# Gradient pass of a gated block: group tiles by parity, one store per weight and group, one sum over both parts of a parameter block

## The chip, the core and the metric

The kernel runs on one core of a Trainium2 chip. The metric is the time of one execution on the device in microseconds (us), taken as the median of several runs. The engines are named as in the profile: PE (TensorE, matrix multiplications; PEld is its weight load), DVE (VectorE), ACT (ScalarE), POOL (GpSimd) and SP (SyncE). POOL and SP do little arithmetic of their own here; they issue transfers (DMAs), and SP also issues transfers that transpose on the way. Each engine runs its own list of instructions in order and waits for others by semaphores. SBUF is the memory on the chip for tiles of 128 partitions, PSUM holds the results of matmuls, and tensors that are too large for them lie in DRAM.

## The reference

The kernel computes the forward pass of a block and the gradients of it with respect to 12 inputs. The input x has 2048 rows of 576 columns. The block is

```
xn = layernorm(x)
s  = conv(xn, K(A, B, C, dt)) + xn * Dskip     # state space model, as a convolution of length 2048
h  = silu(xn @ w1) * (xn @ w3)                 # 2048 x 4608
g  = silu(h @ w2)                              # 2048 x 576
out = x + s * g
```

K is a sum over 128 complex states per column, K[d, l] = Re sum_n C[d,n] exp(dt[d] A[d,n] l) dt[d] B[d,n]. The convolution is done with Fourier transforms as matrix products. Given grad_out, the outputs are out and the gradients of x, of the parameters A, B, C (real and imaginary parts), of log_dt and Dskip, and of w1, w3 and w2. With go the gradient at h @ w2, and G, U the stored xn @ w1 and xn @ w3, the part around the change is

```
gh = go @ w2.T
gu = gh * silu(G);   gg = gh * silu'(G) * U;   h = silu(G) * U
grad w2 = h.T @ go;  grad w1 = xn.T @ gg;      grad w3 = xn.T @ gu
grad xn += gg @ w1.T + gu @ w3.T
```

## The kernel before

All rows are cut into LT = 16 row tiles of 128, the 576 columns into four full chunks of 128 (nfull) and a rest of 64 (rem), and the 4608 hidden columns into NG = 18 groups of FG = 256. The program is written with tile pools: a pool gives out a fixed number of buffers (bufs) for each name, in turn, and a tile whose buffer is still in use waits for its last user. Pools lie in SBUF from the left or, with side="right", from the right, and a pool opened after another was closed may lie over the old one's place; its first writers then wait for the last readers there. The order of instructions on each engine is set by a priority: at(us) (L83) sets it for what follows, and of the instructions of each engine the smaller number goes first as far as dependences allow. So stages are interleaved by numbers given in the code, not by their place in it.

The stages, with their place in the profiled run:

- Up to about 678 us: layer norm, the convolution kernel and the forward convolution, and ffn_hidden (L725), which writes G, U and h to DRAM (G_dram, U_dram by POOL's queue, H_dram by SP's).
- 678 to 832 us: ffn_output (L800). For each row tile it loads h transposed and x_t, go_t, s_t, multiplies by w2 into two PSUM buffers po (L830), takes the sigmoid sgo on ACT (L835), and on DVE makes out, the gradient go_o and the gradient gs of s, which goes to GS_dram. PE then transposes go_o (ptr, L869), and ACT copies it to goT and goTt. Its pools o_ep and o_in lie on the left.
- 832 to about 1720 us: the groups. phase6_load (L1176) allocates and loads w2T, gg_n and h_n for a group, one group ahead, and makes silu and its derivative on ACT and two products on DVE, in quarters of a tile. phase6_group (L1201) computes ph = gh (L1220), copies it on ACT (gh, L1223), multiplies gu_n and gg_n by it on DVE (L1226), computes the gradient of w2 (phase6_grad2, matmuls L1247, copy L1251), stores gu_n and gg_n to GU_dram and GG_dram (L1232, 512 KB each, POOL's queue), and computes the gradients of w1 and w3 (phase6_grad13): for each of the two and each of the four chunks 16 matmuls into pgw (L1265), a copy to gw on ACT (L1268) and a store of 128x256 elements on POOL's queue (L1269); then a tail for the last 64 columns of both at once (L1272 to L1279).
- Beside the groups, to about 1300 us: ssm_bwd_conv (L875), the backward convolution in four quarters (conv_bwd_quarter, L916). It loads gs, multiplies it by xn for the gradient of Dskip (gsxn, L943), and makes spectra and inverse transforms (idft_tile, L596), whose first rows are halved before (L968).
- Beside the groups and the stage after them, 1300 to about 1940 us: ssm_bwd_params (L896), 36 blocks of 16 columns. param_load (L1001) brings qT, pz and the gz tiles on SP's queue two blocks ahead; param_chunk (L1013) runs small matmuls (L1023) into four PSUM tiles T of 128x512 and, for each of them and each of two parts s, one multiplication by pz into pr_q on DVE (L1030) and one sum into S_all (L1033).
- 1720 to 2065 us: phase6_inputs (L1281), the x stage. gg and gu are loaded transposed as ggc and guc, and the weights as wTB, on SP's queue, and multiplied into px (L1308). phase5_final (L1037) makes the parameter gradients from S_all beside it.

Of the kernel before, what the change touches and what calls it, by code (L numbers as in the profile page):

```python
# [11 lines left out]
ALU = mybir.AluOpType  # L12
AX = mybir.AxisListType
FP32 = mybir.dt.float32
BF16 = mybir.dt.bfloat16
I32 = mybir.dt.int32
P = 128
# [43 lines left out]
class K:  # L61
# [534 lines left out]
    def idft_tile(self, pt, V, oc, extra=()):  # L596
        nc, KT = self.nc, self.cfg.KT
        Q, Wq = V.shape[1], V.shape[4]
        sl = slice(oc * P, (oc + 1) * P)
        n = 2 * KT + len(extra)  # L600
        i = 0
        pv = pt[:, 0:Q * Wq].rearrange("p (q d) -> p q d", q=Q)
        for kt in range(KT):
            for ri, mat in enumerate((self.dC, self.dSi)):
                nc.tensor.matmul(pv, lhsT=mat[:, kt, sl], rhs=V[:, :, ri, kt, :], start=(i == 0), stop=(i == n - 1))
                i += 1
        for (lw, rh, o, w) in extra:
            nc.tensor.matmul(pt[:, o:o + w], lhsT=lw, rhs=rh, start=False, stop=(i == n - 1))
            i += 1
# [190 lines left out]
    def ffn_output(self, T0, TB):  # L800
# [11 lines left out]
        with self.tc.tile_pool(name="o_ep", bufs=2) as ep, \  # L812
                self.tc.tile_pool(name="o_in", bufs=2) as ip, \
# [61 lines left out]
    def ssm_bwd_conv(self, T0, TQ, ps):  # L875
# [3 lines left out]
        with self.tc.tile_pool(name="b_k", bufs=1, side="right") as kp, self.tc.tile_pool(name="b_z", bufs=2, side="right") as zp:  # L879
# [4 lines left out]
            nc.vector.tensor_scalar(out=self.lcol[:], in0=self.lcol[:], scalar1=1.0 / 512, scalar2=None, op0=ALU.mult)  # L884
            self.ones_col = kp.tile([P, 1], BF16, name="ones_col")
# [30 lines left out]
    def conv_bwd_quarter(self, g, kp, zp, ps, T0, TQ):  # L916
# [22 lines left out]
        for b in range(NB):  # L939
            prod = zp.tile([P, KT, W], BF16, name="gsxn")  # L940
            for tt in range(KT):
                t = b * KT + tt
                nc.vector.tensor_tensor(out=prod[:, tt, :].rearrange("p (h d) -> p h d", h=2),  # L943
                                        in0=gs[:, t, :].rearrange("p (h d) -> p h d", h=2),
                                        in1=self.nat4(self.xn_bf[:, t, :])[:, g], op=ALU.mult)
            for tt in range(KT):
                nc.tensor.matmul(gds[0:1, 0:W], lhsT=self.ones_col[:], rhs=prod[:, tt, :], start=(b == 0 and tt == 0),
                                 stop=(b == NB - 1 and tt == KT - 1))
# [7 lines left out]
        for i in range(NB - 1, -1, -1):  # L956
# [4 lines left out]
            ZZ = zp.tile([P, 1, 2, KT, W], BF16, name="ZZ")  # L961
            if nxt is not None:
                nc.vector.scalar_tensor_tensor(out=fl(ZZ), in0=fl(nxt), scalar=self.sgn[:, 0:1], in1=fl(Z), op0=ALU.mult,
                                               op1=ALU.add)
            else:
                nc.vector.tensor_copy(out=ZZ[:], in_=Z[:])
            nxt = Z
            nc.vector.tensor_scalar(out=ZZ[:, 0, :, 0, :], in0=ZZ[:, 0, :, 0, :], scalar1=self.hrow[:, 0:1], scalar2=None,  # L968
                                    op0=ALU.mult)
            for oc in range(KT):  # L970
                t = i * KT + oc
                pt = ps.tile([P, 512], FP32, name="et_ps")
                self.idft_tile(pt, ZZ, oc)
                for h in range(2):
                    pv = pt[:, h * W // 2:(h + 1) * W // 2].rearrange("p (c d) -> p c d", d=8)
                    nc.scalar.activation(out=st[:, :, 0, :, h, t], in_=pv, func=ACT.Copy, scale=1.0 / 512)
                    nc.scalar.activation(out=st[:, :, 1, :, h, t], in_=pv, func=ACT.Copy, scale=self.lcol[:, t:t + 1])
# [35 lines left out]
    def param_chunk(self, ch, tiles, S_all, qp, ps):  # L1013
# [3 lines left out]
        if True:  # L1017
            for dg in range(2):
# [7 lines left out]
                for h in range(2):  # L1026
                    d0 = h * (D // 2) + ch * 8 + dg * 4
                    for s in range(2):
                        pr = qp.tile([P, 8, 2, AV], FP32, name="pr_q")
                        nc.vector.tensor_tensor(out=pr[:], in0=T[h][:].rearrange("p r d k a -> p (r d) k a"),  # L1030
                                                in1=pz[:, dg, h, s:s + 2].rearrange("p r d a -> p (r d) a")[:, :, None, :]
                                                .to_broadcast([P, 8, 2, AV]), op=ALU.mult)
                        nc.vector.tensor_reduce(out=S_all[:, 2 * s:2 * s + 2, d0:d0 + 4].rearrange("p k d -> p d k"),  # L1033
                                                in_=pr[:].rearrange("p (r d) k a -> p d k r a", r=2), op=ALU.add,
                                                axis=AX.XY)
# [86 lines left out]
    def backward(self, T0, TG, TQ, TC, TX, gctx, mats):  # L1122
# [10 lines left out]
        with ExitStack() as out:  # L1133
            ffn = ExitStack()
            wp = ffn.enter_context(pool(name="e_w", bufs=2))
            inp = ffn.enter_context(pool(name="e_in", bufs=2))
            elp = ffn.enter_context(pool(name="e_el", bufs=3))
            gwp = ffn.enter_context(pool(name="e_gw", bufs=4))
# [37 lines left out]
    def phase6_load(self, gi, T, TG, wp, inp):  # L1176
# [7 lines left out]
        self.nat_transpose(w2T[:], self.W2_dram[gi * FG:(gi + 1) * FG, :])  # L1184
        gg = inp.tile([P, LT, FG], BF16, name="gg_n")
# [67 lines left out]
    def phase6_grad13(self, gi, gg_n, gu_n, gwp, ps_gw):  # L1253
# [7 lines left out]
        for (nat, oname) in ((gu_n, "out_11"), (gg_n, "out_10")):  # L1261
            for c in range(nfull):
# [4 lines left out]
                gw = gwp.tile([P, FG], BF16, name="gw13")  # L1267
                nc.scalar.copy(out=gw[:], in_=pw_[:, 0:FG])  # L1268
                nc.gpsimd.dma_start(out=aps[oname][c * P:(c + 1) * P, fb:fb + FG], in_=gw[:])  # L1269
# [6 lines left out]
        gw = gwp.tile([P, FG], BF16, name="gw13")  # L1276
# [192 lines left out]
```

## Time and profile before

| what | us |
|---|---|
| median of 5 runs (2087.62 to 2099.35) | 2088.8 |
| the profiled execution | 2074.07 |
| its span, first to last instruction | 2072.3 |
| PE busy | 1806.1 (87%) |
| DVE busy | 1511.9 (73%) |
| ACT busy | 965.8 (47%) |
| POOL busy | 514.3 (25%) |

The mean clock that TensorE was granted in the profiled execution is 0.956 of its full one. A row of instruction groups in the profile reads: line, engine, operation, output and inputs by their names, shapes, number of instructions | busy us in all, mean ns of one | idle us of the engine just before them, and the instruction that ended most of that idle time. In a timeline row come the start in us, the duration from the first to the last instruction of the row in us, engine, line, operation, count, and in brackets the idle time before and what released it. Among the rows that touch the change are

```profile
L1268 ACT CAST gw<-pgw 128x256 bf16<-128x256 f32 x144 | 53.3, 380 | 235.6 <-PE pgw L1265 147.3
L1269 POOL DMA_DIRECT2D out_dram<-gw x144 | 78.3, 546 | 189.3 <-ACT gw L1268 175.6
...
GU_dram<-gu_n POOLq DMA_DIRECT2D x36, 512.0 KB, 5.9
GG_dram<-gg_n POOLq DMA_DIRECT2D x36, 512.0 KB, 7.9
```

The last two are transfers: number, size of each, and the median time from issue to landing in us.

### The profile page before, as it was taken

How to read it: one execution, taken by the hardware profiler on the slowest of the kernel's cores; microseconds unless marked ns; L12 is line 12 of the kernel's file. 1: busy time of each engine (PE TensorE's matmuls, PEld its weight loads, DVE VectorE, ACT ScalarE, POOL GpSimd, SP SyncE). 2: the span in 40 equal slices, each digit the busy share in tenths (PEclk: the TensorE clock that was granted, in tenths of full speed). 3: DMA queues.
4: the chain of work that ended last, by engine and by line, in shares of the span. 5: the costliest groups of instructions: out<-in, count | busy, mean ns of one | idle time of the engine just before them, and what ended most of it. 6: DMA issues, size and time to landing. Idle time of an engine off the chain costs nothing.

```text
span 2072.3 us, 40851 instructions
## 1 busy us (share of the span) xinstructions
PE 1806.1 (87%) x16214; PEld 1253.3 (60%) x16214; DVE 1511.9 (73%) x2826; ACT 965.8 (47%) x1732; POOL 514.3 (25%) x718
## 2 busy tenths in 40 slices
PE   2889888989899999689889998889969986699997
PEld 1443333335453777577777777767747775577785
DVE  7459999997783565469595968599778874487862
ACT  1968888885455111574656657334434510000000
POOL 6015566562122211112112212323212220000000
PEclk9898999999999999799999999999989998899998
DMA  6688788877577896636372645799698779999884
GB/s 177 237 277 274 268 278 279 280 264 256 173 270 180 222 214 147 185 113 208 87 221 77 199 132 160 198 254 277 181 171 221 194 189 199 228 219 211 167 183 63
DMA packets 552113, 421.31 MB, mean 203 GB/s; under 512 B 415601, under 2 KB 482353, under 8 KB 547313
## 3 DMA queue, kind: packets, MB, share of 16 engines
q1 hardware_dynamic: 487648, 254.56, 49.3%
q0 software_dynamic: 39632, 147.49, 22.0%
q10 hardware_dynamic: 24640, 16.65, 2.9%
q8 instruction: 127, 2.08, 0.4%
q14 instruction: 66, 0.53, 0.1%
HBM read 135.96 MB, written 196.27 MB: 160 GB/s over the span
## 4 chain that ended last, share of the span: by engine, by line
PE 32%; DVE 23%; issue 16%; DMA 10%; ACT 6%; POOL 4%; SPq 2%; DVEq 0%; POOLq 0%; ACTq 0%
PE px L1308 10%; PE po L830 6%; DMA out_dram<-gw 4%; PE pgw L1265 4%; DVE pr_q L1030 4%; DVE S_all L1033 2%; DVE t_k L503 2%; SPq L1174 2%; PE pgw L1247 2%; DVE m_k L484 2%; PE ph L1220 2%; DVE q_k L490 2%; DMA gg_n<-G_dram 2%; PE et_ps L587 1%; PE pu L767 1%
## 5 line engine op out<-in xcount | busy, mean ns | idle before, releaser
L1265 PEld LDWEIGHTS <-xn_bf 128*128 128x128 bf16 x2304 | 230.0, 100 | 86.9 <-issue 53.4
L1308 PE MATMUL px<-wTB_w,guc 128*128 128x288 bf16 x1152 | 240.5, 290 | 19.2 <-DMA wTB_w<-in_B_w_dram 9.8
L1308 PE MATMUL px<-wTB_w,ggc 128*128 128x288 bf16 x1152 | 241.1, 290 | 18.2 <-DVE pr_q L1030 10.0
L1030 DVE TENSOR_TENSOR pr_q<-et_ps,pz 128x512 f32<-128x512 f32 x288 | 185.6, 682 | 93.4 <-PE et_ps L1023 88.0
L767 PEld LDWEIGHTS <-xnT 128*128 128x128 bf16 x1152 | 102.3, 99 | 173.8 <-issue 78.8
L1033 DVE TENSOR_REDUCE S_all<-pr_q 128x8 f32<-128x512 f32 x288 | 184.3, 678 | 0.2
L1220 PE MATMUL ph<-w2T,goT 128*128 128x256 bf16 x1152 | 174.9, 279 | 5.5 <-DMA w2T<-W_dram 5.5
L1265 PE MATMUL pgw<-gg_n,xn_bf 128*128 128x256 bf16 x1152 | 139.1, 283 | 40.6 <-ACT gw L1268 40.6
L1247 PE MATMUL pgw<-go_o,h_n 128*128 128x288 bf16 x1152 | 160.8, 291 | 9.6 <-DVE h_n L1198 7.5
L767 PE MATMUL pg<-wmB_w,xnT 128*128 128x512 bf16 x576 | 160.8, 388 | 2.9 <-ACT g_t L776 2.0
L1268 ACT CAST gw<-pgw 128x256 bf16<-128x256 f32 x144 | 53.3, 380 | 235.6 <-PE pgw L1265 147.3
L767 PE MATMUL pu<-wmB_w,xnT 128*128 128x512 bf16 x576 | 155.6, 387 | 2.6 <-ACT u_t L777 2.6
L499 POOL COPY pz_k<-p_k 128x256 bf16<-128x256 bf16 x144 | 135.6, 985 | 46.2 <-issue 37.1
L1265 PE MATMUL pgw<-gu_n,xn_bf 128*128 128x256 bf16 x1152 | 137.9, 277 | 8.7 <-ACT gw L1251 4.0
L830 PE MATMUL po<-w2g,hc 128*128 128x288 bf16 x1152 | 143.7, 286 | 1.3 <-ACT u_t L777 1.3
L1308 PEld LDWEIGHTS <-guc 128*128 128x128 bf16 x1152 | 113.8, 99 | 50.5 <-DMA guc<-GU_dram 10.3
L1308 PEld LDWEIGHTS <-ggc 128*128 128x128 bf16 x1152 | 113.6, 99 | 48.1 <-DMA ggc<-GG_dram 11.1
L1247 PEld LDWEIGHTS <-h_n 128*128 128x128 bf16 x1152 | 112.7, 100 | 38.4 <-DVE h_n L1198 7.7
L1220 PEld LDWEIGHTS <-goT 128*128 128x128 bf16 x1152 | 101.0, 99 | 55.0 <-issue 28.0
L830 PEld LDWEIGHTS <-hc 128*128 128x128 bf16 x1152 | 111.5, 98 | 30.3 <-issue 1.7
L1269 POOL DMA_DIRECT2D out_dram<-gw x144 | 78.3, 546 | 189.3 <-ACT gw L1268 175.6
L1354 ACT ACTIVATE t<-gx 128x576 f32<-128x576 f32 x16 | 10.9, 684 | 245.2 <-DVE gx L1318 239.4
(309 smaller groups left out, 3935.1 us busy)
## 6 DMA issues: line engine op xcount, KB each, us to landing
G_dram<-g_t POOLq DMA_DIRECT2D x72, 256.0 KB, 3.9
U_dram<-u_t POOLq DMA_DIRECT2D x72, 256.0 KB, 3.5
H_dram<-h_t SPq DMA_DIRECT2D x72, 256.0 KB, 3.6
Q_dram<-q_k SPq DMA_DIRECT2D x36, 512.0 KB, 4.0
gg_n<-G_dram POOLq DMA_DIRECT2D x18, 1024.0 KB, 5.9
h_n<-U_dram POOLq DMA_DIRECT2D x18, 1024.0 KB, 6.9
GU_dram<-gu_n POOLq DMA_DIRECT2D x36, 512.0 KB, 5.9
GG_dram<-gg_n POOLq DMA_DIRECT2D x36, 512.0 KB, 7.9
```

Of the source, the lines that this page charges most:

```text
L484: nc.vector.tensor_scalar(out=m[:, o:o + 512], in0=pt[:].bitcast(I32), scalar1=(1 << 17) - 1, scalar2=None, op0=ALU.bitwise_and)
L499: nc.gpsimd.tensor_copy(out=pz[:, g, h, 1:3], in_=pv[:, g, h])
L767: nc.tensor.matmul(pt[:], lhsT=xnT[:, c, ts], rhs=wm[w][:, c, :], start=(c == 0 and not first), stop=(c == nfull - 1 and first))
L830: nc.tensor.matmul(po_[:, pi_, 0:pw], lhsT=hc[:, fi, :], rhs=w2[fi][:, po:po + pw], start=(fi == 0), stop=(fi == FT - 1))
L1030: nc.vector.tensor_tensor(out=pr[:], in0=T[h][:].rearrange("p r d k a -> p (r d) k a"), in1=pz[:, dg, h, s:s + 2].rearrange("p r d a -> p ...
L1033: nc.vector.tensor_reduce(out=S_all[:, 2 * s:2 * s + 2, d0:d0 + 4].rearrange("p k d -> p d k"), in_=pr[:].rearrange("p (r d) k a -> p d k ...
L1220: nc.tensor.matmul(ph[j][:, k, :], lhsT=lw, rhs=rh, start=(n == 0), stop=(n == nfull))
L1247: nc.tensor.matmul(pgw[pi_][:, 0:pw], lhsT=hn[:, tt, fl * P:(fl + 1) * P], rhs=go_o[:, tt, po:po + pw], start=(tt == 0), stop=(tt == LT - 1))
L1265: nc.tensor.matmul(pw_[:, 0:FG], lhsT=self.xn_bf[:, tt, c * P:(c + 1) * P], rhs=nat[:, tt, :], start=(tt == 0), stop=(tt == LT - 1))
L1268: nc.scalar.copy(out=gw[:], in_=pw_[:, 0:FG])
L1269: nc.gpsimd.dma_start(out=aps[oname][c * P:(c + 1) * P, fb:fb + FG], in_=gw[:])
L1308: nc.tensor.matmul(px[pi_][:, 0:pw], lhsT=act[:, fi, :], rhs=wT[p][ai][:, fi - f0, po:po + pw], start=(fi == 0 and ai == 0), stop=(fi == F ...
```

## The change

The change has five parts, all in or before the backward pass.

1. In phase6_grad13 the four chunks of a weight are copied into one tile of 128 x 4 x 256, and one store takes it to DRAM. The tail has its own name, gw13t. The pool e_gw has two buffers for each name instead of four.
2. The pool e_in with two buffers for each of gg_n, h_n and gu_n becomes two pools with one buffer each, one for even and one for odd groups.
3. The pools o_ep and o_in of ffn_output move to the right side.
4. In param_chunk there is one multiplication for each part r of T, which makes the products with both parts of pz that belong to it, and then one sum over the 1024 products of both; pr_q has one buffer.
5. In conv_bwd_quarter four row tiles are multiplied by one instruction; the halving of the first rows moves from the data into two matrices dCh and dSih that are made once, and the copy of Z for the last block goes.

```diff
-    def idft_tile(self, pt, V, oc, extra=()):
+    def idft_tile(self, pt, V, oc, extra=(), half=False):
...
-                nc.tensor.matmul(pv, lhsT=mat[:, kt, sl], rhs=V[:, :, ri, kt, :], start=(i == 0), stop=(i == n - 1))
+                lw = self.half_mats[ri][:, sl] if half and kt == 0 else mat[:, kt, sl]
+                nc.tensor.matmul(pv, lhsT=lw, rhs=V[:, :, ri, kt, :], start=(i == 0), stop=(i == n - 1))
...
-        with self.tc.tile_pool(name="o_ep", bufs=2) as ep, \
-                self.tc.tile_pool(name="o_in", bufs=2) as ip, \
+        with self.tc.tile_pool(name="o_ep", bufs=2, side="right") as ep, \
+                self.tc.tile_pool(name="o_in", bufs=2, side="right") as ip, \
...
+            self.half_mats = []
+            for n, m in (("dCh", self.dC), ("dSih", self.dSi)):
+                mh = kp.tile([P, m.shape[2]], BF16, name=n)
+                nc.vector.tensor_scalar(out=mh[:], in0=m[:, 0, :], scalar1=self.hrow[:, 0:1], scalar2=None, op0=ALU.mult)
+                self.half_mats.append(mh)
...
-            for tt in range(KT):
-                t = b * KT + tt
-                nc.vector.tensor_tensor(out=prod[:, tt, :].rearrange("p (h d) -> p h d", h=2),
-                                        in0=gs[:, t, :].rearrange("p (h d) -> p h d", h=2),
-                                        in1=self.nat4(self.xn_bf[:, t, :])[:, g], op=ALU.mult)
+            nc.vector.tensor_tensor(out=prod[:].rearrange("p t (h d) -> p t h d", h=2),
+                                    in0=gs[:, b * KT:(b + 1) * KT, :].rearrange("p t (h d) -> p t h d", h=2),
+                                    in1=self.xn_bf[:, b * KT:(b + 1) * KT, :].rearrange(
+                                        "p t (h g d) -> p g t h d", h=2, g=4)[:, g], op=ALU.mult)
...
-            ZZ = zp.tile([P, 1, 2, KT, W], BF16, name="ZZ")
+            ZZ = Z
             if nxt is not None:
+                ZZ = zp.tile([P, 1, 2, KT, W], BF16, name="ZZ")
...
-            else:
-                nc.vector.tensor_copy(out=ZZ[:], in_=Z[:])
             nxt = Z
-            nc.vector.tensor_scalar(out=ZZ[:, 0, :, 0, :], in0=ZZ[:, 0, :, 0, :], scalar1=self.hrow[:, 0:1], scalar2=None,
-                                    op0=ALU.mult)
...
-                    for s in range(2):
-                        pr = qp.tile([P, 8, 2, AV], FP32, name="pr_q")
-                        nc.vector.tensor_tensor(out=pr[:], in0=T[h][:].rearrange("p r d k a -> p (r d) k a"),
-                                                in1=pz[:, dg, h, s:s + 2].rearrange("p r d a -> p (r d) a")[:, :, None, :]
+                    pr = qp.tile([P, 2, 2, 8, AV], FP32, name="pr_q", bufs=1)
+                    for r in range(2):
+                        nc.vector.tensor_tensor(out=pr[:, r].rearrange("p k m a -> p m k a"),
+                                                in0=T[h][:, r][:, None].to_broadcast([P, 2, 4, 2, AV]),
+                                                in1=pz[:, dg, h, r:r + 2].rearrange("p s d a -> p (s d) a")[:, :, None, :]
                                                 .to_broadcast([P, 8, 2, AV]), op=ALU.mult)
-                        nc.vector.tensor_reduce(out=S_all[:, 2 * s:2 * s + 2, d0:d0 + 4].rearrange("p k d -> p d k"),
-                                                in_=pr[:].rearrange("p (r d) k a -> p d k r a", r=2), op=ALU.add,
-                                                axis=AX.XY)
+                    nc.vector.tensor_reduce(out=S_all[:, :, d0:d0 + 4].rearrange("p (s k) d -> p k s d", k=2),
+                                            in_=pr[:].rearrange("p r k (s d) a -> p k s d r a", s=2), op=ALU.add,
+                                            axis=AX.XY)
...
-            inp = ffn.enter_context(pool(name="e_in", bufs=2))
+            inp = [ffn.enter_context(pool(name=f"e_in{k}", bufs=1)) for k in range(2)]
             elp = ffn.enter_context(pool(name="e_el", bufs=3))
-            gwp = ffn.enter_context(pool(name="e_gw", bufs=4))
+            gwp = ffn.enter_context(pool(name="e_gw", bufs=2))
...
+        inp = inp[gi % 2]
         gg = inp.tile([P, LT, FG], BF16, name="gg_n")
...
+            gw = gwp.tile([P, nfull, FG], BF16, name="gw13")
             for c in range(nfull):
                 pw_ = ps_gw.tile([P, 512], FP32, name="pgw")
...
-                gw = gwp.tile([P, FG], BF16, name="gw13")
-                nc.scalar.copy(out=gw[:], in_=pw_[:, 0:FG])
-                nc.gpsimd.dma_start(out=aps[oname][c * P:(c + 1) * P, fb:fb + FG], in_=gw[:])
+                nc.scalar.copy(out=gw[:, c, :], in_=pw_[:, 0:FG])
+            nc.gpsimd.dma_start(out=aps[oname][0:nfull * P, fb:fb + FG].rearrange("(c p) f -> p c f", p=P), in_=gw[:])
...
-        gw = gwp.tile([P, FG], BF16, name="gw13")
+        gw = gwp.tile([P, FG], BF16, name="gw13t")
```

## The prediction

> **What bounds the kernel now.** I read the busy shares first, then the engines beside each other by stage, then the chain of waits, then TensorE's waits alone, and last the order of instructions around the places that the change touches. From the page of the profiled run:
>
> ```profile
> span 2072.3 us, 40851 instructions
> PE   2889888989899999689889998889969986699997
> ...
> PE 32%; DVE 23%; issue 16%; DMA 10%; ACT 6%; POOL 4%; SPq 2%; DVEq 0%; POOLq 0%; ACTq 0%
> ...
> L1030 DVE TENSOR_TENSOR pr_q<-et_ps,pz 128x512 f32<-128x512 f32 x288 | 185.6, 682 | 93.4 <-PE et_ps L1023 88.0
> L1033 DVE TENSOR_REDUCE S_all<-pr_q 128x8 f32<-128x512 f32 x288 | 184.3, 678 | 0.2
> ...
> L1265 PE MATMUL pgw<-gg_n,xn_bf 128*128 128x256 bf16 x1152 | 139.1, 283 | 40.6 <-ACT gw L1268 40.6
> ```
>
> PE is busy for 1806.1 us (87%). The change takes no matmul away, so what it can win lies in PE's idle time. By stretches, PE is busy 405.0 of 450 us from 850 to 1300 (gradient groups beside the convolution quarters), 365.3 of 420 from 1300 to 1720 (groups beside parameter blocks) and 193.4 of 225 from 1720 to 1945 (x stage beside parameter blocks). DVE is busy 326.0 of the middle 420, so it is the next engine. PE's own waits from 860 to 1765, as line, line waited for, total us, times, longest:
>
> ```profile
> PE pgw L1265 <- ACT gw L1268: 41.9, 15, 15.3
> PE ph L1220 <- ACT gh L1223: 17.2, 15, 2.0
> PE px L1308 <- DMA wTB_w<-in_B_w_dram: 13.4, 4, 4.7
> ```
>
> The first line is the largest that one part of the change aims at. It names ACT, but ACT's own waits in that stretch say what held the copy:
>
> ```profile
> ACT gw L1268 <- DMA out_dram<-gw: 85.1, 18, 18.0
> ```
>
> The copy of a finished product waits for the store of an earlier one, to have its buffer back. The chain of waits has "DMA out_dram<-gw" with 4% of the span, the same thing. Of PE's 41.9 us, 4.5 belong to the last group, 9.7 lie before 1300, 27.7 after.
>
> **The change, part by part.**
>
> *Stores by weight and group.* Now each of 18 groups makes 8 copies of 128x256 with a store of 64 KB each over four buffers shared with the tail copy; a copy waits for the store four copies earlier, which in the worst case is queued behind the 2 MB of GU and GG stores of the same group (median landing 5.9 and 7.9 us for each 512 KB). After it, four copies fill one tile and one store follows; two tiles in turn, so a copy waits for a store of the group before, some 45 us earlier. Against that the 41.9 us wait has no cause left; what is late next are the matmul chains themselves, DVE's gu_n (3.3 us of PE's waits now) and the tail. The last group's 4.5 us are lost, as the stage behind it is held by transfers: gross 37.4. I keep 90% of the 9.7 before 1300 (PE has little other idle time there) and 70% of the 27.7 after it, where DVE stands at 78% and the DMA share at 86%: 8.7 + 19.4 = **-28** (ends -10 and -37). POOL issues 108 stores fewer at 546 ns, 59 us, and it was busy 25%: nothing on the path.
>
> A rule of the Trainium skill would add to this. "DMA: Bandwidth & Descriptors" (Bandwidth) says to batch transfers; its loads take 0.95 us for 64 KB and 6.15 for 1 MB, so about 2.0 for 256 KB between them, an estimate. Four stores in one would spare 1.8 us of transfer, 36 times 65 us in all, some 5% of the DMA share in the group stage. Here, though, each stored row stays 512 B, so one store moves the same rows as four, and the trace shows a store's landing set by what is queued ahead of it. I count nothing for cheaper transfers; by the rule the 27.7 us after 1300 would go too, -36 instead of -28 for this part.
>
> *Loads by parity, and the side of the output stage's pools.* In the order of instructions of the two built programs, the output pools' move frees the group tiles' place, so that group 0's w2T, gg and h_n are loaded at the start of the output stage (about 685) instead of at its end (836). The seam in PE's order now:
>
> ```profile
> 831.29 0.85 PE L869 MATMUL ptr<-ident_bf,go_o 128*128 128x128 bf16 x5 [4.65 <-DVE go_o L844]
> 837.67 1.01 PE L1220 MATMUL ph<-w2T,goT 128*128 128x256 bf16 x4 [5.52 <-DMA w2T<-W_dram]
> ...
> 853.33 1.62 PE L1247 MATMUL pgw<-go_o,h_n 128*128 128x288 bf16 x6 [7.48 <-DVE h_n L1198]
> ```
>
> 4.65 + 5.52 + 7.48 = 17.65 us idle. With w2T and h_n long there, the second and third go, and 23 ph matmuls (279 ns, 6.4 us) stand in front of the last ptr. The gs load behind the last GS store stays as late as it was (first L587 at 840.17), so I take **-14** (ends -8 and -17.6).
>
> The cost stands at the other end. Group 0's silu work now sits in ACT's queue around the first sigmoids:
>
> ```profile
> 686.93 0.65 ACT L835 ACTIVATE sgo<-po 128x576 f32<-128x576 f32 x1 [3.85 <-PE po L830]
> 695.75 0.65 ACT L835 ACTIVATE sgo<-po 128x576 f32<-128x576 f32 x1 [8.17 <-PE po L830]
> ```
>
> The first sgo now stands behind a silu that waits for gg: the last H store, then 1 MB of G. The last stores land about 682 to 685, the load takes 5.9 to 8, one silu quarter 1.06 and a table load 1.28 on either side: sgo(0) near 696 instead of 687. Queued behind it are DVE's g, e, go_o of tile 0 and, with two po buffers, PE's po of tile 2, due near 696; DVE needs some 4 us after sgo to free po(0). So PE stalls 4 to 5 us, once: **+5** (ends 0 and +12). Three more table loads go in among later sgo. "ScalarE: Activation LUTs" (What ACT_TABLE_LOAD costs) speaks against that: 2.66 us a switch with its drain, 8 us for three. The trace has 1.28 us for one at 844.27 and work at 845.56, so 3.8; either way ACT waited 8.17 us for each sgo, which covers it. By the rule sgo(0) would come 2.8 us later; it is inside the +12.
>
> x_t, go_t and s_t of the first two tiles move up in POOL's queue ahead of the last nine or ten G and U stores, and s_t waits for an S store near 640-646. The store of 634.9 goes to about 648; with three buffers in front of it that is 0 to +3; I take 0, as PE's slice there is not full.
>
> *One multiply per part and one sum over both.* A block of 8 columns now takes TT, reduce, TT, reduce (in fact DVE runs two of each in a row):
>
> ```profile
> 1684.54 1.27 DVE L1033 TENSOR_REDUCE S_all<-pr_q 128x8 f32<-128x512 f32 x2
> 1685.73 1.28 DVE L1030 TENSOR_TENSOR pr_q<-et_ps,pz 128x512 f32<-128x512 f32 x2
> 1686.92 1.27 DVE L1033 TENSOR_REDUCE S_all<-pr_q 128x8 f32<-128x512 f32 x2
> ...
> 1968.93 0.29 DVE L320 TENSOR_TENSOR Wi_c<-Wi_c,Wt 128x128 f32<-128x128 f32 x1
> 1969.26 0.29 DVE L321 TENSOR_SCALAR Wi_c<-Wi_c,dt_col 128x128 f32<-128x128 f32 x1
> ```
>
> The pitch is 1.19 us for two, 2.38 for a tile of 144. After it: two TT of the same size (1.19) and one reduce over 1024. No row shows that reduce; 128 wide independent operations have a pitch of 0.20 and 512 wide ones 0.595, so 1.03 ns an element and 0.595 + 0.53 = 1.12. Sum 2.31, which saves 0.07 a tile. But pr_q has one buffer: the reduce waits for the multiply right before it, and the next multiply for the reduce. The last two lines above are such a pair: pitch 0.33 against 0.20, so 0.13 a hand-off and 2.56 a tile. "VectorE: DVE Perf Modes" (The DRAIN you can't avoid) says instead that a semaphore after each operation costs nothing: -0.07 x 144 = -10 us of DVE. By the row it is +0.18 x 144 = +26. The row decides: 95 of the 144 tiles (190 of 288 TT) lie in 1300-1720, where other group operations now stand between multiply and reduce and hide part of it, and 49 in the x stage. There DVE idles 94 and 72 us, 57.6 and 30.4 of it waiting for PE's L1023, so this cost is covered: 0 (ends -5 and +10). If DVE had no idle time it would be the +26.
>
> *Scale in the matrix, products in one.* 64 TT of 225 ns become 16 of four times the width; 16 scalings (290 ns) and 4 copies (454 ns) go, two 128x512 scalings come, once. Some 10 us of DVE over four quarters, while PE seldom waits there for DVE (et_ps L587 3.1 us, through ACT): **-1** (ends 0 and -3).
>
> *x stage.* Three guc/ggc transposes move behind the 20 of wTB on SP's queue and one more set of gz, qT, pz ahead. SP issues back to back there and the DMA share is 1.03; PE waits 15.6 us for wTB, 10.0 for pr_q, 5.6 for guc. wTB some 2 us earlier, guc some 4 later: **+2** (ends -4 and +8).
>
> **Sum**: -28 - 14 + 5 - 1 + 2 = **-36**. The profiled run took 2074.1 us with 2072.3 of span; -36 makes 2038. The median shown is 2088.8, 14.7 above the profiled one, with the same program; I carry the difference over: **2053**.
>
> **Rivals.** What counts as no change is 0.5%, 10.4 us: 2078.4 to 2099.2. *More comes*: all of the 37.4 and 17.6, no stall at the sigmoid: -55, 2034. For it: 85 us of ACT's waits go. Against: PE's other small waits (ph on gh 17.2) stay.
>
> *Absorbed*: after 1300 transfers are the limit, the wait is renamed (h_n, gu_n or qT late) and the 19.4 stays away; the sigmoid costs 12 rather than 5: -36 + 19 + 7 = -10, and some of x: 2081. For it: DMA share 0.86; the longest wait (15.3 us) fell into a stretch in which a GU store took 20 us. Against: PE hardly waits for qT or h_n today.
>
> *Slower*: DVE's new order in 1300-1720. The group's gu_n/gg_n products (L1226) now stand between a multiply and its reduce, so they queue behind a multiply that waits for PE's L1023; PE's pgw waits for those products. Such waits are 57.6 us in 10, 5.8 each. One for each of the 8.5 groups there is 49 us: -36 + 49 = +13, 2102. From 5.4 us a group on it is slower by over 0.5%. Against: PE now waits only 3.3 us for gu_n.
>
> **Chances.** Forecast 0.50, more 0.17, absorbed 0.16, slower 0.17. The absorbed case lies near the border: faster 0.68, same 0.15, slower 0.17. The range 2030 to 2094 takes the absorbed case and the near part of the slower one.
>
> **What would show it.** PE's "pgw <- ACT gw L1268" falls from 41.9 to under 8; the seam at 830-853 has under 5 us idle; sgo(0) starts near 696 and PE has one gap of about 5 us in 690-705; DVE's tile takes 2.5 to 2.6 us where nothing stands between. Wrong if "pgw <- DVE gu_n" grows to tens of us, if DVE's reduce of 1024 is far above 1.2 us, or if the output stage loses over 12.

## The result, and the profile after

The changed kernel takes 2081.24 us (median of 41 runs) against 2096.06 us of the kernel before (76 runs). The ratio is 0.9916, with a 95% interval of 0.9896 to 0.9937, so it is faster by 0.84% or some 18 us; a second comparison (e5) gave 0.9905 (0.9863 to 0.9946). The forecast was -36 us, to 2053. The sign was right and the size twice too large. Of the distance in absolute time, 7 us come from the starting point: the five runs of the kernel before that were shown had a median of 2088.8, all 76 have 2096.06. Single executions of the changed kernel range from 2052 to 2117 us; the ratio is taken over its fast ones, to which the execution profiled with the result (2088 us) doesn't belong, so a second profile of the same kernel (e5) stands beside it.

The page of the second profile of the changed kernel (lines moved by 1 to 4):

```profile
span 2062.5 us, 40349 instructions
PE   2888988989899699989999999889997985698997
...
L1032 DVE TENSOR_TENSOR pr_q<-et_ps,pz 128x512 f32<-128x512 f32 x288 | 186.5, 687 | 65.0 <-PE et_ps L1025 52.9
L1036 DVE TENSOR_REDUCE S_all<-pr_q 128x16 f32<-128x1024 f32 x144 | 175.4, 1218 | 2.3
...
L1270 PE MATMUL pgw<-gg_n,xn_bf 128*128 128x256 bf16 x1152 | 129.4, 273 | 0.0
```

The pgw row of gg_n, which had 40.6 us of idle time before it, has none now. PE's waits from 860 to 1765 us in the same profile (line, line waited for, us in all, times, longest):

```profile
PE et_ps L1025 <- DVE pr_q L1032: 26.6, 7, 13.2
PE px L1312 <- DMA wTB_w<-in_B_w_dram: 24.2, 4, 13.7
PE et_ps L606 <- ACT gk_st L979: 17.4, 18, 3.1
PE px L1312 <- DMA ggc<-GG_dram: 12.4, 1, 12.4
...
PE pgw L1270 <- ACT gw L1272: 0.4, 2, 0.2
```

The wait at which the stores aimed fell from 41.9 to 0.4 us, as forecast. (The 41.9 us are of one execution: a second profile of the kernel before, e13, has 28.5.) A new one heads the list: PE's small matmuls of the parameter blocks wait for DVE to free a PSUM tile, 26.6 us, where before it was 3.9.

How long each stage takes says more. The program order is fixed, so the same instruction can be found in each profile: the start of the last sigmoid (the output stage's end), the end of a group (its tail copy), the first ggc transfer (the x stage's first), the first gx addition (its first row tile), the end. In us:

| profile | last sigmoid at | to end of group 0 | groups 1-8 | to first ggc | to first gx | to the end |
|---|---|---|---|---|---|---|
| before | 826.3 | 62.5 | 435.7 | 367.3 | 81.3 | 299.2 |
| before, again (e13) | 831.6 | 62.8 | 436.7 | 354.3 | 88.0 | 299.6 |
| changed | 829.9 | 41.6 | 417.4 | 405.3 | 88.1 | 303.6 |
| changed, again (e5) | 837.8 | 41.6 | 417.7 | 360.1 | 89.2 | 316.0 |
| stores alone (e1) | 837.6 | 61.7 | 424.1 | 375.0 | 88.0 | 300.2 |
| parity and sides alone (e2) | 840.1 | 43.3 | 436.2 | 376.1 | 88.9 | 300.5 |
| part 4 alone (e3) | 833.7 | 61.2 | 436.0 | 379.1 | 90.1 | 305.1 |
| part 4 undone (e4) | 841.5 | 42.0 | 421.2 | 359.3 | 82.5 | 312.3 |
| part 4 undone (e6) | 834.1 | 43.8 | 419.6 | 373.4 | 86.4 | 316.2 |
| part 4 undone, stores swapped (e16) | 844.5 | 43.5 | 416.8 | 357.0 | 85.6 | 302.2 |

The second and third columns of times repeat within 1 to 5 us and can be read from one profile. The stretch to the first ggc, where groups and parameter blocks run side by side, differs by 13 us between two executions of the kernel before and by 45 between two of the changed one. Both profiled executions of the kernel before took 2074 us, where its times range from 2068 to 2135, so whole spans must not be subtracted.

The table holds the result: 40 us are gained from the last sigmoid to the end of group 8, and behind it nothing more is won. By the whole time, some 18 us, part of that lead is given back; the last sigmoid itself comes some 8 us later, and the stretches behind group 8 vary too much between executions to say where the rest goes.

### The profile page after: what moved, and what is told of

The parts are those of the page before. It is cut to its first block, busy times and chain, and to the rows that moved or that the text cites. A ratio compares the mean times of both kernels' runs of the same rounds, so it can differ in the third digit from the quotient of the medians.

```text
span 2085.9 us, 40349 instructions
## 1 busy us (share of the span) xinstructions
PE 1796.7 (86%) x16214; PEld 1247.5 (60%) x16214; DVE 1505.3 (72%) x2616; ACT 970.3 (47%) x1735; POOL 467.4 (22%) x610
## 3 DMA queue, kind: packets, MB, share of 16 engines
q0 software_dynamic: 37904, 147.48, 22.5%
## 5 line engine op out<-in xcount | busy, mean ns | idle before, releaser
L1270 PEld LDWEIGHTS <-xn_bf 128*128 128x128 bf16 x2304 | 224.3, 98 | 29.4 <-issue 2.6
L1224 PE MATMUL ph<-w2T,goT 128*128 128x256 bf16 x1152 | 180.2, 288 | 20.7 <-ACT gh L1227 18.7
L1036 DVE TENSOR_REDUCE S_all<-pr_q 128x16 f32<-128x1024 f32 x144 | 175.1, 1216 | 2.3
L499 POOL COPY pz_k<-p_k 128x256 bf16<-128x256 bf16 x144 | 139.8, 1013 | 46.3 <-issue 37.2
L1230 DVE TENSOR_TENSOR gu_n<-gh,gu_n 128x1024 bf16<-128x1024 bf16 x72 | 49.4, 686 | 129.4 <-ACT gh L1227 129.4
L1270 PE MATMUL pgw<-gu_n,xn_bf 128*128 128x256 bf16 x1152 | 132.8, 272 | 1.5 <-ACT gw L1255 1.1
L1270 PE MATMUL pgw<-gg_n,xn_bf 128*128 128x256 bf16 x1152 | 129.4, 273 | 0.0
```

What stands on the lines that cost most here:

```text
L499: nc.gpsimd.tensor_copy(out=pz[:, g, h, 1:3], in_=pv[:, g, h])
L1036: nc.vector.tensor_reduce(out=S_all[:, :, d0:d0 + 4].rearrange("p (s k) d -> p k s d", k=2), in_=pr[:].rearrange("p r k (s d) a -> p k s d ...
L1224: nc.tensor.matmul(ph[j][:, k, :], lhsT=lw, rhs=rh, start=(n == 0), stop=(n == nfull))
L1230: nc.vector.tensor_tensor(out=pair(t_)[:, :, sl], in0=gh[:], in1=pair(t_)[:, :, sl], op=ALU.mult)
L1270: nc.tensor.matmul(pw_[:, 0:FG], lhsT=self.xn_bf[:, tt, c * P:(c + 1) * P], rhs=nat[:, tt, :], start=(tt == 0), stop=(tt == LT - 1))
```

## The experiments

**e1, e2, e3: single parts on the kernel before. e4: the changed kernel without part 4.** The edits are the hunks of the diff in front: for e1 those of phase6_grad13 and e_gw; for e2 those of o_ep, o_in and e_in; for e3 those of param_chunk; e4 takes these last ones back.

> The kernel before with part 1 alone (one tile and one store per weight and group). If the stores hold PE as read (41.9 us of waits, gone in the profile after): the wait of pgw on gw under 2 us; the end of group 8 comes 10 us (predicted) to 18 us (all of the gain that the profile after shows between the ends of groups 0 and 8) earlier. Theory A (the merged sum's order on DVE gives the gain back behind 1300): the x stage starts 30 us earlier, time -25 to -35 us, ratio 0.983 to 0.988. Theory B (transfers limit the stretch behind 1300, whatever DVE does): the lead at 1300 is gone by the x stage, time -8 to +3 us, ratio 0.996 to 1.002.

> The kernel before with parts 2 and 3 alone (e_in by parity, output pools on the right). Sigmoid of tile 0 some 5 us later, end of group 0 some 17 us earlier than before. Theory A: nothing behind takes it, time -10 to -18 us, ratio 0.991 to 0.995. Theory B: the lead is lost in the stretch behind 1300, ratio 0.997 to 1.003.

> The kernel before with part 4 alone (two multiplications, one sum, one buffer). Theory A: the parameter blocks take longer, PE waits for pr_q some 30 us more, x stage 15 to 40 us later, ratio 1.008 to 1.02. Theory B: DVE idles enough, ratio 0.997 to 1.003. In both a tile of 144 takes 2.64 us where nothing stands between and 2.32 where other work does.

> The changed kernel with part 4 undone. Theory A: the lead of about 35 us at 1300 is kept to the x stage, time 2040 to 2060, ratio to before 0.980 to 0.985. Theory B: the lead is lost behind 1300 as in the changed kernel, ratio 0.989 to 0.995.

Measured, as ratio to the kernel before on the same chip: e1 0.9923 (0.9894 to 0.9952), e2 0.998 (0.9945 to 1.0015), e3 1.0132 (1.006 to 1.0203), e4 0.9889 (0.9833 to 0.9944). Stores alone bring 16 us, part 4 alone costs 28. For part 4 the time is that of theory A (ratio 1.008 to 1.02), but not the wait that was to make it. PE's waits from 1300 to 1800 in e3:

```profile
PE pgw L1266 <- ACT gw L1269: 41.4, 10, 11.5
PE px L1309 <- DMA wTB_w<-in_B_w_dram: 19.1, 4, 8.8
PE et_ps L1023 <- DVE pr_q L1030: 6.7, 5, 3.3
```

The wait for pr_q was expected to grow by some 30 us and grew from 3.9 to 6.7. For the stores and the pools e2 has the ratio of theory B; e1 lies between the two theories, and e4 at the edge of B, while e6, the same kernel again, lies at the edge of A. What decides for B is the stretch behind group 8, which no kernel in the table has clearly shorter than the kernel before. PE's waits from 1300 to 1800 in e1:

```profile
PE px L1308 <- DMA wTB_w<-in_B_w_dram: 25.4, 5, 11.9
PE et_ps L1023 <- DMA qT<-Q_dram: 15.0, 1, 15.0
PE ph L1220 <- ACT gh L1223: 13.2, 8, 4.4
PE pgw L1274 <- issue: 5.5, 1, 5.5
PE et_ps L1023 <- DMA gz<-gK_dram: 5.3, 1, 5.3
PE pgw L1247 <- ACT gw L1251: 5.2, 2, 4.2
PE pgw L1266 <- DVE gu_n L1226: 4.6, 6, 1.4
```

The wait on gw is gone here too, and loads of qT and gz, gh and gw2 stand in its place. Without the px rows the named waits of 1300-1720 came to 55 us in the kernel before (32.2 of them on gw; 45 and 20.2 in e13) and come to 52 here; the stretch to the first ggc takes 375 us against 367 and 354. The wait was renamed, not removed.

**e5, e6, e7, e8: why part 4 costs.** e5 is the changed kernel, e6 has part 4 undone again, both on one chip. The other two edit pr_q alone:

```diff
# e7, in the changed kernel (gw2 and gw13t get bufs=1 for the room)
-                    pr = qp.tile([P, 2, 2, 8, AV], FP32, name="pr_q", bufs=1)
+                    pr = qp.tile([P, 2, 2, 8, AV], FP32, name="pr_q", bufs=2)
# e8, in the kernel before
-                        pr = qp.tile([P, 8, 2, AV], FP32, name="pr_q")
+                        pr = qp.tile([P, 8, 2, AV], FP32, name="pr_q", bufs=1)
```

> The changed kernel once more, beside the other three on the same chip. Ratio 0.990 to 0.994 as before. If the profile after fell on a poor execution, the stall of 22 us that ACT had there at 1337-1359 behind a late load of gg_n is gone or smaller; the tiles of the parameter blocks should keep their pitch (2.64 us with nothing between, 2.32 with other work between).

> The changed kernel with part 4 undone, again, for its distance to the changed kernel on one chip. Theory A (part 4 costs some 28 us wherever it stands): 20 to 30 us below the changed kernel, ratio to before 0.978 to 0.983. Theory C (part 4 costs only where the stores hold PE as well; with these gone DVE has room): within 10 us of the changed kernel, ratio 0.986 to 0.992.

> The changed kernel with two buffers for pr_q (gw2 and gw13t get one each for the room). Theory A1 (the cost of part 4 is its one buffer, which makes each operation wait for the one right before it and ties the order of DVE): as fast as with part 4 undone or faster, DVE tiles at 2.32 us also where nothing stands between. Theory A2 (the cost is the sum over 1024 and the later freeing of PSUM tiles): as the changed kernel, within 5 us.

> The kernel before with one buffer for pr_q and nothing else: multiply, sum, multiply, sum, each waiting for the one before. Theory A1: a tile takes 2.38 + 4 x 0.13 = 2.9 us where nothing stands between, and the kernel is slower by 15 to 60 us, ratio 1.007 to 1.03. Theory A2: within 0.3% of before.

Measured: e5 0.9905 (0.9863 to 0.9946), e6 0.9798 (0.9725 to 0.9872), e7 1.0133 (1.0056 to 1.021), e8 1.0016 (0.9973 to 1.0059). Part 4 costs about 1.1% on top of the other parts too (the intervals of e5 and e6 just touch), so theory C falls. But theory A1, the single buffer, falls with e8. DVE's own time, in timelines (start, duration, operation, count), first e5, then e8:

```profile
1547.39 1.29 DVE L1032 TENSOR_TENSOR pr_q<-et_ps,pz 128x512 f32<-128x512 f32 x2 [4.59 <-PE et_ps L1025]
1548.72 1.22 DVE L1036 TENSOR_REDUCE S_all<-pr_q 128x16 f32<-128x1024 f32 x1
1550.04 1.29 DVE L1032 TENSOR_TENSOR pr_q<-et_ps,pz 128x512 f32<-128x512 f32 x2
```

```profile
1618.21 0.69 DVE L1030 TENSOR_TENSOR pr_q<-et_ps,pz 128x512 f32<-128x512 f32 x1
1618.94 0.69 DVE L1033 TENSOR_REDUCE S_all<-pr_q 128x8 f32<-128x512 f32 x1
1619.73 0.69 DVE L1030 TENSOR_TENSOR pr_q<-et_ps,pz 128x512 f32<-128x512 f32 x1
...
1621.18 0.69 DVE L1030 TENSOR_TENSOR pr_q<-et_ps,pz 128x512 f32<-128x512 f32 x1
```

A tile of part 4 takes 2.65 us with nothing between (1547.39 to 1550.04). In e8 an operation comes each 0.73 to 0.79 us instead of 0.595, 3.0 us a tile (1618.21 to 1621.18) for the 2.38 of the kernel before, and the kernel is no slower. So, in the kernel before, neither the single buffer nor DVE's longer time is what costs. In e7, which changes three numbers of buffers, the order of the program changed as well: the first row tile of the x stage comes 1001 us after the last sigmoid (905 in e4), behind the parameter blocks instead of beside them, although the groups end as early as in e4 (850 against 847). e7 therefore decides neither about the buffer nor about theory A2, the sum over 1024, which e8 leaves standing; it shows what numbers of buffers can do to the order.

What part 4 does to PE shows in its waits behind 1280 us. The line "et_ps on pr_q" has 39.3 us in the first profile of the changed kernel and 26.6 in e5, against 3.1 in e4 and 1.5 in e6. About half of it is one stall at one place of the program. In e5, from POOL to PE:

```profile
1558.81 0.55 POOL L1192 DMA_DIRECT2D gg_n<-G_dram  x1 [12.20 <-DMA GG_dram<-gg_n]
...
1566.48 1.28 ACT L1197 ACT_TABLE_LOAD   x1 [13.72 <-DMA out_dram<-gw13t]
1567.77 1.06 ACT L1197 ACTIVATE gu_n<-gg_n 128x1024 bf16<-128x1024 bf16 x1
1568.73 0.57 ACT L1227 CAST gh<-ph 128x512 bf16<-128x512 f32 x1
...
1569.33 0.69 DVE L1230 TENSOR_TENSOR gu_n<-gh,gu_n 128x1024 bf16<-128x1024 bf16 x1 [13.22 <-ACT gh L1227]
1569.94 1.28 DVE L1032 TENSOR_TENSOR pr_q<-et_ps,pz 128x512 f32<-128x512 f32 x2
...
1571.28 0.58 PE L1025 MATMUL et_ps<-gz,qT 128*128 128x128 bf16 x4 [13.20 <-DVE pr_q L1032]
```

The gg_n load of the group after next goes into the buffer from which GG was stored, and waited 12.2 us for that store to land. That store stood on POOL's queue behind an h_n load of 1 MB that took 19.9 us, where the median of e5 is 8.6. ACT has the silu of that gg_n in its queue in front of a gh copy; DVE has gu_n, which needs the copy, in front of the multiplication that frees the PSUM tile; PE waits for the tile. A late transfer reaches PE through three queues. Whether that is what part 4 costs is another matter: from the end of group 8 to the first ggc PE is idle for 35 us in e5, with that stall, and for 36 in e4, without it (46 in e6; 78, 51, 41 and 65 in the first profile of the changed kernel, e10, e11 and e12).

**e9, e10, e11, e12: part 5 alone, the order of two stores, and parity undone.** e9 is the hunks of idft_tile and the quarters on the kernel before; e12 takes the pools' hunks back from the changed kernel. e10 and e11 are one kernel, the changed one with

```diff
-        for (dst, t_) in ((self.GU_dram, gu), (self.GG_dram, gg)):
+        for (dst, t_) in ((self.GG_dram, gg), (self.GU_dram, gu)):
```

(the label of e11 names part 4, which is in it; its expectation says what ran).

> The kernel before with part 5 alone (products of four row tiles at once, the halving in the matrices, no copy of Z). The prediction had -1 us; the profile after shows 18 us gained between the ends of groups 0 and 8, of which the stores alone gave 12. Theory D (DVE's and ACT's order in the quarters is looser without the scalings): 6 to 12 us faster, ratio 0.994 to 0.997. Else: 0.999 to 1.001.

> The changed kernel with the GG stores issued ahead of the GU stores. Theory E (with the store waits gone, the next late thing is the chain GG store, gg_n load into the same buffer, silu on ACT in front of the gh copies): POOL's wait of the gg_n load on the GG store and ACT's wait of the silu on gg_n fall from 12-31 and 30-70 us to under half, the groups end 5 to 20 us earlier and the time falls by 3 to 15 us, ratio 0.984 to 0.989. Rival (the x stage is limited by transfers and takes it back): ratio as the changed kernel, 0.990 to 0.992.

> One look more at the same kernel for the spread of single executions: the stall of PE behind the late gg_n at the same place (13.2 and 17.2 us in the two profiles of the changed kernel) under 5 us.

> The changed kernel with parts 2 and 3 undone. The prediction had -9 us for these parts, alone they measured -4 us (-12 to +3). If the same here: ratio 0.993 to 0.996. If the parity pools carry more because loads no longer collide: 0.996 to 1.0.

Measured: e9 0.9882 (0.9824 to 0.9941), e10 0.9886 (0.9835 to 0.9938), e12 0.9883 (0.9821 to 0.9946); e11 was a single execution. The ratio of e10 is within the range of theory E, but its interval takes in the changed kernel's 0.9905 and 0.9916, and the mechanism of E falls: with GG first, the stall at the same place is as long, in e10

```profile
1597.39 0.58 PE L1025 MATMUL et_ps<-gz,qT 128*128 128x128 bf16 x4 [21.87 <-DVE pr_q L1032]
```

and 20.2 us in e11, each behind an h_n load of 24 and 25 us. So the order of the two stores was not what made it long. e9 came out below both of its expected ranges and is not settled: its time says -25 us, but the one profile has the groups 1 to 8 in 439.2 us, 3 us longer than before. Beside the stores part 5 does show: 417 to 421 us in the changed kernel and in e4, 415.8 in e12, 424.1 for the stores alone. e12 missed its expectation too: with the pools as before, the kernel was to lose at least a few us against the changed one and lost nothing, though group 0 again took 62.6 us instead of 41.6. In its profile the stretch behind group 8 took 394 us.

**e13, e14, e15, e16: the transposing loads of the weights.** e13 is the kernel before, for the table above. e14 (changed) and e15 (before) replace ten transposes at 1300-1400 by two plain loads of the same size, which bring other values; e16 is part 4 undone with the two stores swapped.

```diff
-            for (do, dsz) in cfg.dch:
-                self.nat_transpose(t[:, :, do:do + dsz], self.aps[w][do:do + dsz, f0 * P:f1 * P])
+            if f0 == 0:
+                self.nc.sync.dma_start(out=t[:], in_=self.aps["B_w2"][0:f1 * P, :].rearrange("(c p) d -> p c d", p=P))
+            else:
+                for (do, dsz) in cfg.dch:
+                    self.nat_transpose(t[:, :, do:do + dsz], self.aps[w][do:do + dsz, f0 * P:f1 * P])
```

> The kernel before once more, one look, as a second profile to hold the others against. From the end of the output stage (the last sigmoid): the end of group 0 after 62.5 us and of group 8 after 498 us as in the first, within 3; from there the first transfer of the x stage after 367 and the end after another 380, each within some 15 us.

> The changed kernel with the first ten transposing loads of the x stage's weights, which run at 1300-1400, put out by two plain loads of the same size from w2 (so the gradient of x is of other weights). Theory F (behind 1300 the stretch is limited by transfers, and what the stores gave is taken there): from the end of group 8 to the first transfer of the x stage 20 to 50 us less than the 360 to 405 of the changed kernel, no stall of ACT behind gg_n over 10 us there, time 15 to 40 us less. Rival (the order of DVE and PE in part 4 alone sets the stretch): 365 or more, time within 8 us of the changed kernel.

> The same replacement in the kernel before, for what the transposes cost there. Theory F: the stretch 10 to 30 us shorter than the 367 of the kernel before, and with it the waits of pgw on gw behind 1300 (32.2 us) fall to under 20, since the stores land sooner. Rival: 360 to 370, waits as before.

> The changed kernel with part 4 undone and the GG stores ahead of the GU stores. Theory E: some 3 to 10 us below the 2059 to 2067 us of part 4 undone alone, ratio to before 0.976 to 0.984. Rival (the order of the two stores does nothing): 0.980 to 0.989.

Measured: e14 0.986 (0.9804 to 0.9916), e15 0.9942 (0.9902 to 0.9982), e16 0.9851 (0.9792 to 0.9909). e13 fell as expected (499.5 us to the end of group 8, then 354 and 388). The stretch took 371.3 us in e14 and 358.2 in e15, no clear change from 360-405 and 354-367. Theory F is not confirmed as it was put: these transposes cost some 0.6% in the kernel before (in the changed one the difference, 0.5%, is within the interval), but they don't set the length of the stretch. In e15 the waits of pgw on gw fell to 8.9 us (from 32.2 and 20.2 in the two profiles of the kernel before), as expected, and still the stretch was no shorter: once more a wait in that stretch was taken away without a gain. e16 lies in the range of the rival: the order of the two stores does nothing that these runs can tell.

**e17, e18: the transposing loads of qT.** The changed kernel, and the same with part 4 undone, each with plain loads of the same size that bring the factors in another order:

```diff
-        self.nat_transpose(qT[:], self.Q_dram[ch])
+        nc.sync.dma_start(out=qT[:], in_=self.Q_dram[ch].rearrange("(p c) n -> p c n", p=P))
```

> The changed kernel with the 36 transposing loads of qT put out by plain loads of the same size (so the parameter gradients are of permuted factors). Theory G (the stretch behind 1300 and the spread of the changed kernel come from collisions: a load of 1 MB of h_n or gg_n that runs beside a transposing load of qT lands after 17-25 us instead of 6-8, the stores behind it on POOL's queue as late, the next gg_n load waits for the GG store, ACT's silu for gg_n, and with it gh, DVE's products and PE's L1025): no h_n or gg_n load of groups 10 to 17 over 13 us, no stall of PE on pr_q over 5 us, the stretch from the end of group 8 to the first transfer of the x stage under 355 us, ratio to before 0.970 to 0.983. Rival H (part 4 costs by its order on DVE and PE even where nothing collides): stretch 360 or more, ratio 0.985 to 0.992.

> The same replacement with part 4 undone. Theory G: within 8 us of e17, since what part 4 costs is the collisions. Rival H: 15 to 30 us below e17, as far as part 4 undone lies below the changed kernel.

Measured: e17 0.9768 (0.9698 to 0.9839; median 2043.5), e18 0.9692 (0.9612 to 0.9772; median 2019.4). Without those 36 transposes both kernels gain between 1.1 and 2% (against e5, e4 and e6), more than the whole change brought. The two don't agree: part 4 undone stays 16 us (by the ratios) to 24 us (by the medians) below, though here the intervals overlap. PE's waits from 1280 to 1700, first e17, then e18:

```profile
PE et_ps L1025 <- DVE pr_q L1032: 34.8, 6, 23.4
PE et_ps L1025 <- DMA gz<-gK_dram: 6.0, 1, 6.0
```

```profile
PE pgw L1250 <- ACT gw L1254: 13.3, 2, 12.0
PE ph L1223 <- ACT gh L1226: 9.1, 7, 2.0
PE et_ps L1025 <- DMA qT<-Q_dram: 7.5, 2, 6.9
...
PE et_ps L1025 <- DVE pr_q L1032: 1.7, 2, 0.9
```

In e17 two h_n loads still took 21 us and one gg_n load 24, now beside transposes of the weights, and PE's stall of 23.4 us is there again. So the collisions aren't qT's alone (theory G falls in that form), and part 4 keeps its price (rival H, in the distance between the two kernels, though not in e17's ratio). e18 had an h_n load of 20 us too, and one stall of 12 us, at another place.

**The faster version.** Part 4 undone beats both kernels: 0.9889 and 0.9798 against the kernel before in e4 and e6 (12 runs, 2044 to 2082 us), and 0.9851 with the stores swapped. Beside the changed kernel on one chip (e5 with e6) it is 1.1% faster; e4, measured on another chip, lies only 0.2 to 0.3% below the changed kernel's ratios.

## Why the prediction was half right

Two terms of the sum failed. The first is "70% of the 27.7 after it", the 19.4 us that the stores were to bring behind 1300: nothing of them came. The second is part 4, put at 0 because "this cost is covered": it costs 28 us alone and some 16 to 24 beside the other parts. The seam and the groups up to the eighth, on the other side, brought more than forecast, for reasons that the prediction did not have. That the total kept the right sign at half the size is in that measure luck.

*Stores: -28 forecast, -16 alone (e1).* The mechanism was right: the waits on gw went from 41.9 to 0.4 us. Up to group 8 the size held: 12 us (424.1 against 436) for 8.7. Behind 1300 it failed. The stretch to the first ggc takes 354 and 367 us in the kernel before and 375, 359, 373 and 357 where the stores are merged and part 4 is not in (e1, e4, e6, e16); PE is idle in it for 32 and 45 us there and for 34 to 48 here. The waits have new names: qT, gz, gh. This is the rival "absorbed". The 41.9 us were also a sample of a quantity that varies: where the stores are as before, e13 has 28.5 and e2 46.0 in the same window. What limits the stretch is not settled; e17 and e18 show that the transposing loads of qT have a large part in the kernel's time. (In the aside on cheaper transfers, 65 us are 7% of the 888 us of the group stage, not 5; nothing was counted for it.)

*Seam: -14 forecast, -21 measured* (62.5 to 41.6). The idle time went as read: 17.65 us were counted, and some 15 of the 19 us of idle time in this stretch are gone. Another 5 us the prediction did not have: the same matmuls run faster. The stretch in the kernel before and in e5 (window, length, busy us of PE, PEld, DVE, ACT and POOL with their instructions, then PE's granted clock, DMA share, GB/s):

```profile
826.30:888.80 62.50, 43.80 (x363) 33.20 (x361) 25.08 (x56) 33.49 (x57) 11.82 (x20) 0.81 0.60 182
837.80:879.40 41.60, 38.34 (x362) 30.38 (x360) 19.95 (x44) 23.40 (x47) 7.93 (x12) 1.00 0.66 203
```

A ph matmul takes 315 ns in the mean of the first and 274 in the second. In all 8 profiles with the pools as before this stretch has 17 to 20 us of idle time and a clock of 0.78 to 0.84, in the 12 with the moved pools 3 to 5 us and 0.96 to 1.00. The gs load that was to stay late fell behind other work: L587 starts at 849.51 in e5, and no wait of it over 1.2 us is left.

*Sigmoid: +5 forecast, some +8 measured.* PE waits for tile 0 at the place foreseen, but for longer than the 4 to 5 us. The first profile of the changed kernel, then e5, then e13, the kernel before:

```profile
697.35 0.85 PE L870 MATMUL ptr<-ident_bf,go_o 128*128 128x128 bf16 x5 [8.78 <-DVE go_o L845]
705.02 0.85 PE L870 MATMUL ptr<-ident_bf,go_o 128*128 128x128 bf16 x5 [20.38 <-DVE go_o L845]
699.35 0.85 PE L869 MATMUL ptr<-ident_bf,go_o 128*128 128x128 bf16 x5 [7.58 <-DVE go_o L844]
```

The third line shows that such a gap isn't the pools' alone: 4 of the 8 profiles with the pools as before have one, of 7.6 to 11.4 us, and 4 have none. With the moved pools all 12 have one, of 3.5 to 20.4 us. The means, 4.7 and 12.5, are 8 us apart, and so are those of the last sigmoid: 838.2 and 830.3 us, inside the 0 to 12. What the wait follows is seen in e5, where the first sigmoid stands behind the silu and a table load, at 700.06 instead of 686.93:

```profile
697.69 1.06 ACT L1197 ACTIVATE gu_n<-gg_n 128x1024 bf16<-128x1024 bf16 x1 [31.09 <-issue]
698.76 1.28 ACT L836 ACT_TABLE_LOAD   x1
700.06 0.65 ACT L836 ACTIVATE sgo<-po 128x576 f32<-128x576 f32 x1
```

The table load takes 1.28 us and the work behind it starts at once, so the row and not the 2.66 us of the Trainium skill ("ScalarE: Activation LUTs", What ACT_TABLE_LOAD costs) held. In whole times seam and sigmoid together don't show: alone they measured -4 us (e2, -12 to +3), and the changed kernel without them was no slower (e12).

*Part 4: 0 forecast, 28 us alone.* The arithmetic of DVE held: 2.65 us a tile for the 2.56 worked out, and 2.33 with other work between (in the first profile 3.53 us from one to the next, with two products of 0.60 us between) for 2.31. For the hand-off, the dependent pair's row was nearer than the rule of "VectorE: DVE Perf Modes" (The DRAIN you can't avoid) that a semaphore costs nothing: in e8 an operation that waits for the one before comes 0.13 us later or more. DVE's longer time is covered, as said (e8, 3.0 us a tile at no loss). What failed is the step from there to 0: DVE's time was counted, and nothing for the new order of the work. With merged stores the order shows in PE's wait for DVE's release of PSUM tiles, 19 to 39 us in the seven profiles with part 4 and one buffer (both of the changed kernel, e10, e11, e12, e14, e17) and 3.1 or less where part 4 is undone (e4, e6, e16, e18). But that this wait is the cost is not shown: alone (e3) part 4 costs most with 6.7 us of it, and e5 has no more idle time in the stretch than e4. The cause of part 4's cost stays open between the order and the sum over 1024. The rival "slower" had the right neighbours, L1226 among the multiplications and sums, and the wait the other way round: not the product behind a multiplication, but a multiplication behind a product that waits for ACT, in one long stall and not one in each group.

*Part 5: -1 forecast.* The groups 1 to 8 gained 18 us, the stores alone 12, so more than the 1 us comes from elsewhere: with the stores and part 5 in they gained 14 (e4) and 20 (e12). e9 was to show it alone and did not settle it.

*x stage: +2 forecast.* From the first ggc to the first gx it takes 80 to 91 us in all kernels but e7 (174), so this stage passes a lead on but adds nothing. Its rest takes 299 us in both profiles of the kernel before and 304 and 316 in the changed one; with part 5 alone it was 317, so a loss of some 10 us can't be laid on the order of SP's queue.

Together: 40 us won from the last sigmoid to group 8 for 23.7 forecast there, 8 lost at the sigmoid for 5, and instead of another 19 us a part of the lead given back behind.

## What to carry to other kernels

When a wait is taken off an engine, look at which wait ends next in the same stretch, and credit the gain only where the stretch gets shorter; a wait that was the last of several late things is merely renamed. Cost a change of buffers not by its instructions alone but ask also what order it gives to each engine: a product that waits for a late load, in front of the operation that frees another engine's buffer, carries the lateness to that engine. And before a span or a wait is subtracted from another, take a second profile of the same kernel: pieces that repeat within 2 us can be compared, the others can't.

## What the runs showed of the hardware

A 1 MB load (h_n) lands 8.6 us after its issue in the median of e5 and 6.9 in that of the kernel before. In the same kernels, at some places, it takes 17 to 25 us, and what stands behind it on its queue is as late: in e5 the 512 KB stores behind one took 20.9 and 22.5 us. That load (issued at 1530.96, landed at 1550.84) ran beside a transposing load on SP's queue that had been issued at 1530.36 and small loads of gz at 1529.22; a like one in e4, with none of them issued within 5 us, took 6.3. The kernel before has such a load in one of its two profiles (25 us) and not in the other (6 us). That transposes are the cause was not shown: with those of qT taken out, two such loads remained.
